# Layer norm's exact root on GpSimd instead of VectorE, and a new written order for all steps

## The chip, the cores and the metric

The kernel runs on one core of one Trainium2 chip. The metric is the device time of one execution in microseconds (us). Three runs of the kernel before took 794.92, 795.9 and 796.6 us; the median is 795.9 us.

Names used below: PE is TensorE (PEld its weight load), DVE is VectorE, ACT is ScalarE, POOL is GpSimd, SP is SyncE, whose queue issues nearly all the transfers of this kernel. A small q behind an engine's name (SPq) is its sequencer, which waits and issues.

## The reference

Inputs are q, k and v (8 x 8 heads x 576 x 64), a gain g of 512 and two matrices, 512 x 2048 and 2048 x 512.

```python
k_p = k.reshape(B, H, S // 8, 8, D).mean(axis=3)          # pooled keys and values
v_p = v.reshape(B, H, S // 8, 8, D).mean(axis=3)
scores = (q @ k_p.T) / sqrt(D);  attn = softmax(scores);  x = attn @ v_p
mu = mean(x);  var = mean((x - mu)**2)                     # rows of 512
xn = (x - mu) / np.sqrt(var + 1e-06) * g_ln                # layer norm
out = x + np.maximum(xn @ w_ch1, 0.0) @ w_ch2              # feed-forward
```

The random inputs give scores with a large spread (q and k are multiplied by 8), so float32 accuracy is kept: large products are made of float16 parts (high and low).

## The kernel before, in words

**Tiles and chunks.** The 4608 rows are 36 tiles of 128 rows; four tiles make a chunk of 512 rows, and there are nine chunks, 0 to 8. Scores, softmax and values of a tile are the steps A and B. The feed-forward of a chunk follows: for chunks 0 and 1 by plain products (steps I, lines 1083 to 1098, and O, lines 1118 to 1135), for chunks 2 to 8 by a Strassen scheme with seven products (steps U, whose matmuls are line 794, and E, whose matmuls are line 1017). The parts that these products read are made by ACT (high part) and by DVE or POOL (low part: source minus high part; lines 839 and 846 among others).

**The root.** Layer norm's 1/sqrt is found in two parts. For each tile the last part of step B (lines 627 to 644) makes the variance `ve_all` and a first guess `s_all` by integer arithmetic, and the row is scaled with the guess. The correction to the exact root, times the output scale, is found for four tiles at once by step NR (`norm_scale`, line 558): from 128x4 tiles, one instruction after the other, each reading what the one before it wrote, into `cr`. The second product's accumulation (lines 1033 and 1129, on DVE) multiplies by `cr`. So NR of a chunk may run at any time between the chunk's last step B and its first accumulation. In the kernel before NR has eight instructions on DVE (lines 563 to 580), in three pieces with a `yield` between.

**Low parts on POOL.** POOL makes part of the low parts (lines 545, 548, 679, 702, 846), half of the weight forms (lines 741, 744, 949, 952) and a conversion (line 347).

**Transfers.** SP's queue takes them in order. A doubled copy of the values (`va`, `vb`, lines 428 and 429, four transfers for each batch) is read by the matmuls of step B (lines 596 and 597). `vr` (line 405) and `kr` (line 401) have one buffer each, so a load waits until DVE has reduced the one before it (lines 1172 and 1148).

**The order.** Nothing is left to a scheduler: the string `START` is a list of 2486 tokens, and each token runs one step up to its next `yield`. `NR.4`, for one, appears three times in it: a piece each. Each engine's queue, and SP's, gets its instructions in the order in which the tokens issue them, and keeps to it; semaphores make an instruction wait for another engine's.

```python
    def step(token):
        if token not in begun:
            name, *args = token.split(".")
            begun[token] = iter(ops[name](*map(int, args)) or ())
        next(begun[token], None)

    with tc.manual_schedule():
        for token in START.split():
            step(token)
```

Of the kernel before, what the change touches and what calls it, by code (L numbers as in the profile page):

```python
# [63 lines left out]
C.2.0.1.1 K.1 V.1 K.1 C.1.4.1 K.1 K.1 B.2 B.3 K.1 C.2.0.1.1 C.1.4.1 R.1.5 K.1 A.4 S.1.2 C.1.4.1 V.1 A.4 C.2.0.1.1
R.2.6 S.1.3 S.1.3 A.5 B.2 C.1.4.1 C.1.5.1 C.1.5.1 A.4 B.2 B.3 I.0.0.0 A.4 B.3 C.1.5.1 A.4 B.2 I.0.0.0 HV.2.0 A.5 B.3
HK.2.0 C.2.6.1 C.2.6.1 R.2.2 B.2 C.1.5.1 A.5 A.4 HK.2.1 B.3 C.2.6.1 I.0.0.0 I.0.0.0 R.2.4 A.4 C.2.2.1.1 I.0.1.1
I.0.0.0 I.0.1.0 I.0.1.1 M1.1 M1.1 C.2.6.1 A.5 C.2.2.1.1 C.2.2.1.1 I.0.0.0 I.0.1.0 B.4 M1.1 V.1 A.5 I.0.1.1 S.1.4
C.2.2.1.1 I.0.0.0 A.6 A.6 I.0.1.0 V.1 I.0.1.0 I.0.0.0 B.4 I.0.1.0 C.2.4.1 A.6 I.0.1.1 I.0.1.1 S.1.4 S.1.5 I.0.0.0
I.0.0.1 I.0.0.1 R.2.3 V.1 C.2.3.1 I.0.1.0 HV.2.0 HK.2.1 A.5 A.5 A.6 S.1.5 I.0.0.1 I.0.0.1 I.0.0.1 C.2.3.1 R.2.5
C.2.3.1 QS.9 A.6 I.0.0.1 HK.2.0 C.2.4.1 C.2.4.1 I.0.1.1 A.7 I.0.1.1 I.0.1.1 S.1.6 I.0.1.1 C.2.3.1 S.1.6 I.0.0.1  # L70
I.0.0.1 I.0.1.1 HK.2.0 I.0.0.1 V.1 V.1 I.0.0.0 I.0.0.1 I.0.0.0 S.1.7 S.1.7 I.0.2 B.4 I.0.0.1 I.0.0.0 I.0.0.1 A.6
HV.2.1 HV.2.1 C.2.5.1.1 A.7 C.2.5.1.1 C.2.5.1.1 C.2.4.1 I.0.1.1 I.0.2 I.0.1.1 R.2.1 I.0.1.0 I.0.1.0 B.4 HK.2.1 HV.3.1
QS.9 I.0.2 C.2.5.1.1 A.7 T.0.0.1 HV.3.1 I.0.1.0 I.0.3 B.5 T.0.0.1 I.0.1.0 NR.0 I.0.3 R.2.7 C.2.1.1 C.2.1.1 I.0.3
I.0.1.0 T.0.0.1 B.5 C.2.7.1 B.4 I.0.2 I.0.2 I.0.3 C.2.1.1 B.4 A.6 C.2.7.1 C.2.7.1 T.0.0.1 C.2.1.1 I.0.1.0 HK.2.1 I.0.2
I.0.2 C.2.7.1 A.7 T.0.0.1 M2 X.0 I.0.2 T.0.0.1 HV.2.0 HV.2.0 X.1 M2 I.0.3 A.8 B.5 M2 I.0.3 I.0.2 S.2.0 A.8 I.0.2 B.4
I.0.2 S.2.0 KS.2 I.0.3 Y.0 T.0.0.1 HV.2.0 Y.1 A.7 S.2.1 I.0.2 S.2.1 I.0.3 S.2.2 KS.2 HV.2.0 I.0.3 S.2.2 X.2 HV.2.0
S.2.3 I.0.3 I.0.3 T.0.0.1 F.0.0.0 S.2.3 HV.2.0 I.0.3 Y.2 A.8 S.2.4 QS.9 QS.9 A.7 QS.10 KS.2 KS.2 NR.0 S.2.4 T.0.0.1
NR.0 B.5 B.6 HV.3.1 S.2.5 B.5 F.0.0.0 S.2.5 X.3 T.0.0.1 HV.3.1 HK.3.0 HV.3.1 QS.9 O.0.0 O.0.0 T.0.0.1 F.0.0.0 B.5 Y.3
F.0.0.0 O.0.0 QS.9 S.2.6 S.2.6 S.2.7 HV.3.1 KS.2 S.2.7 O.0.0 O.0.0 A.8 B.6 T.1.0.1 B.7 B.5 B.7 B.6 KS.2 HV.3.1 A.8 B.7
T.1.0.1 O.0.0 B.6 QS.10 T.0.0.1 B.7 HV.3.1 QS.10 B.6 B.6 N.1.1 F.0.0.0 O.0.0 QS.10 QS.10 B.7 O.0.1 A.9 O.0.1 A.9 A.9  # L80
A.8 HV.2.1 B.6 B.7 B.7 F.0.0.0 B.4 QS.12 HK.3.0 QS.10 HV.2.1 HK.3.0 T.0.0.1 A.9 F.0.0.0 HV.2.1 F.0.0.0 O.0.1 O.0.1
O.0.1 O.0.1 F.0.0.0 F.0.0.0 O.0.0 O.0.1 HV.2.1 F.0.0.0 B.8 HV.2.1 A.10 A.10 QS.11 I.1.0 A.9 I.1.0 O.0.1 A.10 HV.2.1
HV.2.1 B.8 T.1.0.1 T.1.0.1 A.9 HK.3.0 I.1.3 I.1.0 F.0.1.1 HV.2.1 F.0.1.1 HV.3.0 A.10 T.1.0.1 I.1.2 F.0.0.0 HV.2.1
HV.3.0 QS.11 QS.11 HK.3.1 O.0.1 O.0.1 HV.3.0 QS.11 F.0.1.1 HK.3.1 HV.3.0 HK.3.1 F.1.0.1 F.1.0.1 T.1.0.1 I.1.3 B.8
I.1.3 I.1.2 QS.11 I.1.3 F.1.0.1 I.1.2 A.10 NR.1 HV.2.1 I.1.3 HV.3.0 HV.3.0 I.1.3 QS.11 F.1.0.1 F.1.0.1 N.0.1 F.1.0.1
I.1.1 A.10 F.1.0.1 HV.2.1 HV.2.1 T.1.0.1 HK.3.1 N.1.3 O.0.1 O.0.1 I.1.3 F.1.0.1 KS.3 I.1.3 A.11 A.11 I.1.0 F.0.1.1
I.1.3 A.11 QS.12 HV.3.0 KS.3 KS.3 I.1.1 A.11 QS.12 I.1.1 QS.13 I.1.1 B.8 QS.12 QS.12 B.10 B.10 F.1.0.1 KS.3 F.1.0.1
HV.3.0 NR.1 T.1.0.1 I.1.0 A.11 I.1.0 F.1.0.1 QS.13 I.1.1 QS.13 I.1.0 I.1.1 I.1.0 I.1.0 I.1.2 I.1.3 KS.3 F.1.1.0 A.11
I.1.2 I.1.2 F.1.1.0 QS.13 B.10 T.1.0.1 KS.3 F.1.0.1 T.1.0.1 F.1.1.0 HV.4.1 I.1.0 I.1.0 I.1.1 B.8 QS.13 F.2.0.0 F.2.0.0
F.1.1.0 I.1.1 B.9 B.9 B.8 I.1.3 HV.4.1 B.9 I.1.1 I.1.1 QS.12 T.0.1.1 N.0.2 I.1.0 NR.1 HV.4.1 I.1.2 B.9 A.12 T.0.1.1  # L90
QS.13 F.2.0.0 A.12 N.1.0 T.1.0.1 A.12 HV.4.1 I.1.1 B.11 B.9 QS.15 I.1.3 I.1.2 I.1.1 T.0.1.1 HV.4.1 QS.14 T.1.0.1 B.10
B.9 F.2.0.0 O.1.0 F.2.0.0 HV.4.1 I.1.2 A.12 A.13 I.1.2 B.11 B.8 QS.14 QS.14 B.9 O.1.0 B.9 F.2.0.0 F.2.0.0 HK.4.0 QS.14
HV.4.1 B.9 B.9 A.12 QS.14 B.11 HK.4.0 F.2.0.0 QS.14 B.9 HV.3.1 HK.4.0 F.2.0.0 F.2.0.0 HV.4.1 QS.15 O.1.0 HV.4.0 A.12
O.1.0 B.11 F.2.0.0 I.1.2 T.1.0.1 T.1.1 B.9 QS.15 QS.15 N.0.3 O.1.0 A.14 O.1.0 B.9 HV.4.0 O.1.0 NR.2 F.2.1.1 HV.4.0
QS.15 QS.15 B.11 T.0.1.1 I.1.2 HK.4.0 O.1.1 B.10 QS.16 B.10 B.11 F.2.1.1 B.11 A.13 A.13 F.2.1.1 B.10 F.2.1.1 O.1.1
HK.4.1 O.1.1 O.1.1 F.3.0.1 B.12 U.2.0.1 T.1.1 B.11 B.11 O.1.0 A.14 NR.2 HV.4.0 F.3.0.1 HK.4.1 F.2.0.0 B.11 B.11 O.1.1
B.12 A.13 F.3.0.1 N.1.2 F.3.0.1 F.3.0.1 HV.4.0 QS.16 B.11 T.1.1 O.1.1 HV.3.1 HV.3.1 O.1.1 O.1.1 B.12 B.11 F.3.0.1
T.0.1.1 O.1.1 F.3.0.1 HV.4.0 U.2.0.1 B.12 F.3.0.1 HK.4.1 T.1.1 F.3.0.1 F.3.0.1 T.1.1 QS.16 QS.16 A.15 F.3.0.1 A.13
O.1.1 U.2.0.6 O.1.1 HK.4.1 U.2.0.6 U.2.0.6 U.2.0.2 U.2.0.5 U.2.0.7 F.3.0.1 U.2.0.2 F.3.1.0 QS.16 HV.3.1 U.2.0.2 A.13
HV.4.0 N.0.0 U.2.0.5 U.2.0.3 U.2.0.7 U.2.0.4 HV.3.1 U.2.1.1 NR.2 U.2.0.3 U.2.0.7 A.14 U.2.1.1 HV.3.1 U.2.0.7 U.2.1.6  # L100
A.14 B.13 HV.4.0 J.1.0 U.2.0.4 U.2.0.3 U.2.1.6 B.13 U.2.2.1 J.0.1 U.2.0.3 F.3.1.0 F.3.1.0 D.2.0.0 U.2.1.6 U.2.0.4
U.2.0.3 U.2.0.4 HV.4.1 U.2.1.2 U.2.0.3 U.2.1.7 QS.17 U.2.1.5 F.3.1.0 U.2.2.1 U.2.1.2 U.2.1.2 U.2.2.2 B.13 U.2.1.5
HV.5.0 HK.5.0 A.15 U.2.1.3 U.2.1.7 U.2.1.4 U.2.0.4 U.2.0.4 U.2.0.4 J.0.0 QS.16 B.12 U.2.1.3 HV.4.1 HV.5.0 KS.4 HV.4.1
U.2.0.4 U.2.1.3 E.2.0.1 U.2.1.7 U.2.1.4 U.2.1.3 E.2.0.1 U.2.1.4 U.2.2.6 KS.4 U.2.2.6 KS.4 A.14 D.2.0.1 U.2.1.4 U.2.1.4
KS.4 A.14 E.2.0.2 E.2.0.2 A.16 QS.18 HV.5.0 U.2.1.4 E.2.0.6 U.2.2.5 O.1.1 A.15 U.2.1.4 U.2.1.4 U.2.2.6 D.2.0.2 QS.17
QS.17 QS.17 U.2.1.3 KS.4 U.2.2.2 QS.17 B.13 U.2.2.7 U.2.2.2 A.15 QS.18 HK.5.0 J.1.1 U.2.1.3 U.2.2.5 B.13 E.2.0.6 B.14
E.2.0.5 A.16 E.2.0.6 D.2.0.3 U.2.2.7 U.2.2.4 U.2.2.7 QS.18 A.15 A.15 HK.5.1 A.16 B.12 B.14 B.14 U.2.2.4 U.2.2.3 QS.18
QS.18 B.13 E.2.0.7 B.15 U.2.2.7 U.2.2.3 U.2.2.4 U.2.1.7 E.2.0.5 U.2.3.1 U.2.2.4 U.2.3.1 HV.4.1 E.2.0.3 U.2.3.6 HK.5.1
# [1260 lines left out]
```

## Time and profile before

| | us |
|---|---|
| three runs | 794.92, 795.9, 796.6 |
| the profiled execution | 795.79 |
| its span (first to last instruction) | 794.0 |
| PE busy | 769.4 (97%) |
| DVE busy | 683.0 (86%) |
| ACT busy | 501.7 (63%) |
| POOL busy | 322.0 (41%) |

The span is 1.8 us shorter than the execution's own time. Matmul ends are modelled, so PE's busy time is not all peak work. A group's row in a list by line and form gives the line, engine, operation, output and inputs, shapes and count, then the busy time (us) and the mean duration (ns), then the idle time of the engine just before and what ended it. A mean that is larger than that of a sister group with the same shape is time in which the instruction had started and was held up.

### The profile page before, as it was taken

How to read it: one execution, taken by the hardware profiler on the slowest of the kernel's cores; microseconds unless marked ns; L12 is line 12 of the kernel's file. 1: busy time of each engine (PE TensorE's matmuls, PEld its weight loads, DVE VectorE, ACT ScalarE, POOL GpSimd, SP SyncE). 2: the span in 40 equal slices, each digit the busy share in tenths (PEclk: the TensorE clock that was granted, in tenths of full speed). 3: DMA queues.
4: the chain of work that ended last, by engine and by line, in shares of the span. 5: the costliest groups of instructions: out<-in, count | busy, mean ns of one | idle time of the engine just before them, and what ended most of it. 6: DMA issues, size and time to landing. Idle time of an engine off the chain costs nothing.

```text
span 794.0 us, 17760 instructions
## 1 busy us (share of the span) xinstructions
PE 769.4 (97%) x6904; PEld 618.0 (78%) x6904; DVE 683.0 (86%) x1439; ACT 501.7 (63%) x963; POOL 322.0 (41%) x282
## 2 busy tenths in 40 slices
...
GB/s 332 355 276 272 227 279 219 216 196 128 137 199 192 279 136 207 193 181 145 177 158 220 91 182 163 177 138 176 208 89 154 111 140 127 118 148 89 27 108 120
DMA packets 248356, 140.72 MB, mean 177 GB/s; under 512 B 158112, under 2 KB 225680, under 8 KB 245200
## 3 DMA queue, kind: packets, MB, share of 16 engines
...
q10 hardware_dynamic: 144, 0.13, 0.0%
...
## 4 chain that ended last, share of the span: by engine, by line
PE 70%; DVE 22%; DMA 3%; ACT 2%; issue 2%; SPq 1%; POOL 0%; DVEq 0%; ACTq 0%
PE ps_f L1017 29%; PE ps_f L794 28%; PE ps_f L1083 4%; DMA vr<-in_v_dram 2%; DVE vp L1172 1%; DVE w L315 1%; PE ps_f L1118 1%; PE ps_f L1272 1%; PE ps L486 1%; DVE w L353 1%; DVE ring L1097 1%; DMA w<-in_vn_dram 1%; PE ps_f L1256 1%; PE ps L594 1%; DVE ring L846 1%
## 5 line engine op out<-in xcount | busy, mean ns | idle before, releaser
L1017 PE MATMUL ps_f<-w,ring 128*128 128x256 f16 x2352 | 267.6, 273 | 4.3 <-DVE ring L839 1.9
L1017 PEld LDWEIGHTS <-ring 128*128 128x128 f16 x2352 | 229.0, 98 | 31.9 <-issue 4.3
L794 PE MATMUL ps_f<-zz,w 128*128 128x256 f16 x1344 | 160.6, 273 | 0.0
L794 PEld LDWEIGHTS <-w 128*128 128x128 f16 x1344 | 130.5, 98 | 15.0
L846 POOL TENSOR_TENSOR ring<-v,ring 128x512 f16<-128x512 f32 x56 | 67.0, 1200 | 166.1 <-ACT ring L843 149.1
L794 PE MATMUL ps_f<-zz,raw 128*128 128x256 f16 x1008 | 121.8, 273 | 0.5 <-DVE v L902 0.4
L794 PEld LDWEIGHTS <-raw 128*128 128x128 f16 x1008 | 97.7, 98 | 12.5 <-issue 0.6
L1083 PE MATMUL ps_f<-zz,w 128*128 128x512 f16 (+1 forms) x480 | 88.8, 344 | 3.6 <-DVE ring L1097 3.6
L1118 PE MATMUL ps_f<-w,ring 128*128 128x512 f16 x384 | 84.8, 379 | 0.7 <-DVE ring L1097 0.4
L1083 PEld LDWEIGHTS <-w 128*128 128x128 f16 x480 | 47.3, 100 | 39.4 <-issue 6.2
L1118 PEld LDWEIGHTS <-ring 128*128 128x128 f16 x384 | 36.9, 98 | 45.2 <-DVE ring L1097 1.3
L846 POOL TENSOR_TENSOR ring<-ring 128x512 f16<-128x512 f32 x28 | 34.7, 1241 | 66.4 <-ACT ring L843 49.3
L545 POOL TENSOR_TENSOR phl<-e,phl 128x512 f16<-128x512 f32 x31 | 38.0, 1224 | 50.9 <-ACT phl L537 46.1
L702 POOL TENSOR_TENSOR hl<-z,hl 128x512 f16<-128x512 f32 x28 | 32.7, 1176 | 54.2 <-ACT hl L700 44.5
L622 ACT ACTIVATE x<-ps,rs 128x64 f32<-128x64 f32 x144 | 33.1, 316 | 10.8 <-DVE x L614 10.5
L843 ACT CAST ring<-v 128x512 f16<-128x512 f32 x56 | 34.5, 618 | 5.7 <-DVE v L852 3.9
L843 ACT CAST ring<-ring 128x512 f16<-128x512 f32 x56 | 34.0, 618 | 3.0 <-PE ps_f L1017 2.9
L1172 DVE TENSOR_REDUCE vp<-vr 72x64 f32<-72x512 f32 x48 | 32.3, 674 | 3.1 <-DMA vr<-in_v_dram 3.1
L869 ACT COPY ps_f<-w 128x512 f32<-128x512 f32 x28 | 16.5, 589 | 28.2 <-DVE w L867 28.2
L537 ACT CAST phl<-e 128x1024 f16<-128x1024 f32 x31 | 32.4, 1046 | 2.3 <-DMA pt<-phl 1.3
L1033 DVE SCALAR_TENSOR_TENSOR x<-ps_f,cr,x 128x256 f32<-128x256 f32 x58 | 25.3, 476 | 9.4 <-PE ps_f L1017 9.4
L644 ACT ACTIVATE z<-x,nb,s_all 128x512 f32<-128x512 f32 x36 | 29.2, 815 | 5.9 <-DVE nb L639 5.6
...
## 6 DMA issues: line engine op xcount, KB each, us to landing
...
```

The source lines that it names most:

```text
L537: nc.scalar.copy(out=ph[:, :, :, 0:KA], in_=e[:, :, 0:KA].unsqueeze(1).broadcast_to([P, 2, H, KA]))
L545: nc.gpsimd.tensor_tensor(out=ph[:, 0, :, KA:P], in0=e[:, :, 0:KA], in1=ph[:, 0, :, 0:KA], op=ALU.subtract)
L622: nc.scalar.activation(out=xh[:, 4 + i, :], in_=px[:, 1, i, 0:D], func=AF.Copy, scale=rs[:, 4 + i : 5 + i])
L644: nc.scalar.activation(out=z, in_=x, func=AF.Identity, scale=y, bias=nb)
L702: nc.gpsimd.tensor_tensor(out=hl[:, 1, r], in0=part, in1=hl[:, 0, r], op=ALU.subtract)
L794: nc.tensor.matmul(ps[:, j], lhsT=w_form(wb, int(m == 2), k)[:, fs], rhs=z_form(za, int(m == 1), k), start=(first and i == 0 and j == 0), ...
L843: nc.scalar.copy(out=hi, in_=src)
L846: eng.tensor_tensor(out=lo, in0=src, in1=hi, op=ALU.subtract)
L1017: nc.tensor.matmul(parts[i], lhsT=h[:, hp, f, i * P : (i + 1) * P], rhs=w[:, f // FPB, wp, f % FPB], start=(first and f == k == 0 and (i = ...
L1083: nc.tensor.matmul(ps, lhsT=w[:, part, fs], rhs=zT[:, kz, cols], start=(n == 0), stop=(n == 3 * NKT - 1),)
L1118: nc.tensor.matmul(ps, lhsT=h[:, part, i, cols], rhs=w[:, wp, j], start=(n == 0), stop=(n == 3 * NFT // 2 - 1),)
L1172: nc.vector.tensor_reduce(out=vp[b][:, h, 0:D], in_=vraw.pop((b, h)), axis=AX.X, op=ALU.add,)
```

## The change: NR's arithmetic on POOL, and a new START

The function `norm_scale` issues on POOL what it issued on DVE. [...] The three pieces stay (three, three and four instructions instead of three, two and three). Nine steps NR make 90 POOL instructions. `START` has the same 2486 tokens, each as often as before, in another order over its whole length.

```diff
-LK.0 K.0 Q.1 Q.0 K.0 LV.0 A.1 A.1 A.1 R.1.1 A.1 A.0 R.1.3 V.0 A.1 A.1 G A.0 A.0 V.0 A.0 V.0 C.1.1.0.1 V.0 Q.2 V.0 V.0
+Q.1 LK.0 K.0 K.0 Q.0 LV.0 A.1 A.1 A.1 A.0 A.0 A.1 V.0 A.1 V.0 V.0 A.1 V.0 V.0 R.1.1 C.1.1.0.1 C.1.1.0.1 R.1.3 A.0
...
-        nc.vector.tensor_tensor(out=a, in0=v, in1=y, op=ALU.mult)
-        nc.vector.scalar_tensor_tensor(
-            out=a, in0=a, scalar=2.0 ** (-2 * Z_EXP), in1=y, op0=ALU.mult, op1=ALU.mult
-        )
-        nc.vector.tensor_scalar(
-            out=d, in0=a, scalar1=-0.5, scalar2=1.5, op0=ALU.mult, op1=ALU.add
-        )
-        yield
-        nc.vector.tensor_tensor(out=u, in0=d, in1=d, op=ALU.mult)
-        nc.vector.tensor_tensor(out=u, in0=u, in1=a, op=ALU.mult)
-        yield
-        nc.vector.scalar_tensor_tensor(
-            out=a, in0=u, scalar=10.0 / 3.0, in1=u, op0=ALU.subtract, op1=ALU.mult
-        )
-        nc.vector.scalar_tensor_tensor(
-            out=a, in0=a, scalar=5.0, in1=d, op0=ALU.add, op1=ALU.mult
-        )
-        nc.vector.tensor_scalar(
-            out=cr[:, r], in0=a, scalar1=0.375, scalar2=c_out, op0=ALU.mult, op1=ALU.mult
-        )
+        tt, ts = nc.gpsimd.tensor_tensor, nc.gpsimd.tensor_scalar
+        k = 2.0 ** (-2 * Z_EXP)
+        tt(out=a, in0=v, in1=y, op=ALU.mult)
+        tt(out=a, in0=a, in1=y, op=ALU.mult)
+        ts(out=d, in0=a, scalar1=-0.5 * k, scalar2=1.5, op0=ALU.mult, op1=ALU.add)
+        yield
+        tt(out=u, in0=d, in1=d, op=ALU.mult)
+        tt(out=u, in0=u, in1=a, op=ALU.mult)
+        ts(out=a, in0=u, scalar1=k, scalar2=-10.0 / 3.0, op0=ALU.mult, op1=ALU.add)
+        yield
+        tt(out=a, in0=a, in1=u, op=ALU.mult)
+        ts(out=a, in0=a, scalar1=k, scalar2=5.0, op0=ALU.mult, op1=ALU.add)
+        tt(out=a, in0=a, in1=d, op=ALU.mult)
+        ts(out=cr[:, r], in0=a, scalar1=0.375, scalar2=c_out, op0=ALU.mult, op1=ALU.mult)
```

Behind `norm_scale` every line number of the changed kernel is smaller by 6 (line 846 is 840 there, 1033 is 1027). Three places of the queues follow. In them `m_5243` and `t_5244` (before), `m_5308`, `m_5310` and `t_5309` (changed) are the small tiles of NR.4, and `cr` its result.

DVE's queue before, around the third piece of NR.4 (lines 574, 577 and 580):

```order
L839 SCALAR_TENSOR_TENSOR ring<-v,ring 128x512
L852 SCALAR_TENSOR_TENSOR v<-v,zz 128x512
L902 TENSOR_TENSOR v<-ps_f,v 128x512
L1033 SCALAR_TENSOR_TENSOR x<-ps_f,cr,x 128x256 x2
L574 SCALAR_TENSOR_TENSOR m_5243<-m_5245 128x4
L577 SCALAR_TENSOR_TENSOR m_5243<-m_5243,t_5244 128x4
L580 TENSOR_SCALAR cr<-m_5243,c_out 128x4
L517 TENSOR_TENSOR e<-ps_5484,mx 128x576
L846 TENSOR_TENSOR ring<-ring 128x512
```

The three small instructions stand in DVE's queue between the work of two products; in the changed kernel none of NR is left in this queue.

POOL's queue of the changed kernel, the second and third piece of NR.4:

```order
L840 TENSOR_TENSOR ring<-v,ring 128x512
L569 TENSOR_TENSOR m_5310<-t_5309 128x4
L570 TENSOR_TENSOR m_5310<-m_5310,m_5308 128x4
L571 TENSOR_SCALAR m_5308<-m_5310 128x4
L840 TENSOR_TENSOR ring<-v,ring 128x512
L573 TENSOR_TENSOR m_5308<-m_5308,m_5310 128x4
L574 TENSOR_SCALAR m_5308<-m_5308 128x4
L575 TENSOR_TENSOR m_5308<-m_5308,t_5309 128x4
L576 TENSOR_SCALAR cr<-m_5308,c_out 128x4
L840 TENSOR_TENSOR ring<-v,ring 128x512
```

The small instructions stand between POOL's low parts (line 840 here, 846 before); in the kernel before POOL's queue has none of NR.

SP's queue around the doubled values of batch 2, before:

```order
L405 DMA vr<-in_v_dram 72x512
L472 DMA_TRANSPOSE q<-q 128x8x128
L963 DMA d2T_1315<-v 128x1024
L941 DMA d2B_1852<-w_88 128x4x256
L556 DMA_TRANSPOSE pt<-phl_108 128x16x128
L428 DMA va<-vh 64x520
L429 DMA vb<-vh 8x520
L428 DMA va<-vh 64x520
L429 DMA vb<-vh 8x520
```

and in the changed kernel:

```order
L405 DMA vr<-in_v_dram 72x512
L556 DMA_TRANSPOSE pt<-phl_108 128x16x128
L957 DMA d2T_1498<-v 128x1024
L405 DMA vr<-in_v_dram 72x512
L453 DMA q<-in_qn_dram 128x512
L428 DMA va<-vh 64x520
L429 DMA vb<-vh 8x520
L428 DMA va<-vh 64x520
L429 DMA vb<-vh 8x520
```

There a load of `vr`, which waits for a reduction on DVE (line 1166 of the changed kernel), now stands just ahead of the four transfers.

## Rows read from the trace of the kernel before

**Rows 1.** Windows: stretch, length, busy us (xcount) of PE PEld DVE ACT POOL, clock, DMA share, GB/s.

```profile
20.00:100.00 80.00, 73.62 (x501) 56.26 (x501) 74.52 (x144) 71.03 (x125) 35.13 (x24) 0.85 0.85 282
100.00:240.00 140.00, 138.30 (x841) 67.13 (x840) 128.81 (x258) 75.42 (x144) 93.04 (x66) 1.00 0.77 196
240.00:480.00 240.00, 235.50 (x2411) 207.99 (x2411) 225.07 (x503) 163.94 (x324) 92.54 (x88) 1.00 0.78 178
480.00:620.00 140.00, 139.69 (x1459) 125.35 (x1458) 125.90 (x283) 95.32 (x193) 47.88 (x47) 1.00 0.70 160
```

**Rows 2.** Waits of PE, 100 to 480 us: us in total, times, longest.

```profile
PE ps_f L1017 <- DVE ring L839: 1.9, 2, 1.0
PE ps_f L1017 <- DVE x L1033: 1.0, 1, 1.0
PE ps_f L1017 <- ACT v L1049: 0.9, 1, 0.9
PE ps_f L299 <- DVE rowmax L277: 0.8, 1, 0.8
...
```

**Rows 3.** Lines by form, DVE, 100 to 480 us: NR's eight instructions.

```profile
L571 DVE TENSOR_TENSOR m<-t 128x4 f32<-128x4 f32 x5 | 4.6, 922 | 0.0
L580 DVE TENSOR_SCALAR cr<-m,c_out 128x4 f32<-128x4 f32 x5 | 3.7, 739 | 0.2
L564 DVE SCALAR_TENSOR_TENSOR m<-m,s_all 128x4 f32<-128x4 f32 x5 | 3.0, 604 | 0.2
L567 DVE TENSOR_SCALAR t<-m 128x4 f32<-128x4 f32 x5 | 2.7, 537 | 0.2
L574 DVE SCALAR_TENSOR_TENSOR m<-m 128x4 f32<-128x4 f32 x5 | 2.2, 432 | 0.0
L563 DVE TENSOR_TENSOR m<-ve_all,s_all 128x4 f32<-128x4 f32 x5 | 2.2, 431 | 0.0
L572 DVE TENSOR_TENSOR m<-m,m 128x4 f32<-128x4 f32 x5 | 0.8, 163 | 0.2
L577 DVE SCALAR_TENSOR_TENSOR m<-m,t 128x4 f32<-128x4 f32 x5 | 0.8, 163 | 0.2
```

**Rows 4.** Timeline of DVE at 89, 179 and 726 us: start, length, instruction.

```profile
89.53 0.99 DVE L567 TENSOR_SCALAR t<-m 128x4 f32<-128x4 f32 x1
...
179.28 1.84 DVE L571 TENSOR_TENSOR m<-t 128x4 f32<-128x4 f32 x1
...
725.96 0.15 DVE L571 TENSOR_TENSOR m<-t 128x4 f32<-128x4 f32 x1
```

**Rows 5.** Timeline of POOL, 178 to 183 us.

```profile
178.97 2.13 POOL L741 TENSOR_TENSOR raw<-w,raw 128x1024 f16<-128x1024 f32 x1
```

**Rows 6.** Lines by form, POOL, whole span.

```profile
L846 POOL TENSOR_TENSOR ring<-v,ring 128x512 f16<-128x512 f32 x56 | 67.0, 1200 | 166.1 <-ACT ring L843 149.1 <-DVE m L574 8.7 <-DMA va<-vh 8.2
...
L548 POOL TENSOR_TENSOR phl<-e,phl 128x64 f16<-128x64 f32 x31 | 12.6, 406 | 0.0
...
L250 POOL MEMSET kp_all<- 128x16 f32 x1 | 0.1, 111 | 0.0
```

**Rows 7.** Lines by form, DVE, whole span: first and last of its groups, and line 846.

```profile
L1172 DVE TENSOR_REDUCE vp<-vr 72x64 f32<-72x512 f32 x48 | 32.3, 674 | 3.1 <-DMA vr<-in_v_dram 3.1
...
L846 DVE TENSOR_TENSOR ring<-ring 128x512 f16<-128x512 f32 x28 | 24.8, 887 | 0.5 <-ACT ring L843 0.5
...
L846 DVE TENSOR_TENSOR ring<-zz,ring 128x512 f16<-128x512 f32 x15 | 10.3, 687 | 1.5 <-ACT ring L843 1.4
...
L1276 DVE MEMSET vp<- 72x8 f32 x2 | 0.1, 65 | 0.0
```

**Rows 8.** Instructions of lines 428 and 429 (SP): ns min/median/max, first and last start.

```profile
L428 SPq DMA_DIRECT2D va<-vh x14: 504/516/804, 70.9 to 603.5; - x14
...
L429 SPq DMA_DIRECT2D vb<-vh x14: 670/715/852, 71.5 to 604.0; - x14
```

**Rows 9.** Chain that ended last, 100 to 260 us: start, us, a transfer's part.

```profile
175.03 3.63 DMA vr<-in_v_dram
```

More of the change, by code (lines that the diff above doesn't have):

```diff
@@ L64 @@
[L64 to L108, printed above, removed]
@@ new lines @@
+V.1 HK.2.0 S.1.3 R.2.6 HK.2.1 C.1.5.1 C.1.4.1 C.1.4.1 C.1.4.1 S.1.3 A.4 A.4 I.0.0.0 B.2 C.1.5.1 I.0.0.0 C.2.6.1
+I.0.1.0 B.3 I.0.1.0 A.4 A.4 C.2.6.1 I.0.0.0 C.1.5.1 B.2 I.0.1.0 A.5 I.0.1.0 C.1.5.1 C.2.6.1 A.4 NR.0 V.1 A.5 I.0.1.0
+I.0.1.0 I.0.0.0 A.4 B.4 R.2.2 B.2 C.2.6.1 A.5 A.5 B.2 I.0.1.1 HV.2.0 HK.2.1 C.2.2.1.1 R.2.3 C.2.2.1.1 I.0.0.0 HV.2.0
+M1.1 C.2.2.1.1 A.5 M1.1 M1.1 I.0.1.1 I.0.1.1 A.5 R.2.4 I.0.0.0 I.0.1.1 A.6 A.6 V.1 I.0.1.1 A.6 C.2.3.1 I.0.1.1 I.0.0.0
+A.6 S.1.4 C.2.4.1 C.2.2.1.1 S.1.4 B.4 C.2.3.1 C.2.3.1 I.0.1.0 I.0.1.0 I.0.1.0 I.0.0.1 C.2.4.1 I.0.0.1 I.0.0.1 S.1.5
@@ new lines @@
+A.5 S.1.5 I.0.0.1 I.0.0.1 I.0.0.0 A.6 HK.2.0 HV.2.1 I.0.0.1 C.2.4.1 S.1.6 I.0.0.1 HV.2.1 I.0.0.0 A.7 S.1.6 I.0.1.1
+I.0.0.1 A.7 I.0.1.1 I.0.1.1 I.0.0.1 A.6 I.0.0.1 R.2.5 C.2.3.1 HV.3.1 S.1.7 S.1.7 I.0.0.0 I.0.0.1 QS.9 R.2.1 I.0.0.0
+B.4 V.1 I.0.3 C.2.4.1 HV.3.1 I.0.0.0 C.2.5.1.1 B.4 C.2.5.1.1 C.2.5.1.1 C.2.1.1 I.0.1.1 HK.2.0 V.1 I.0.3 I.0.2 I.0.3
+B.5 R.2.7 I.0.0.1 B.5 QS.9 T.0.0.1 I.0.1.1 I.0.2 C.2.1.1 I.0.1.1 I.0.2 HV.2.0 I.0.1.0 HK.2.1 X.0 T.0.0.1 C.2.7.1
+C.2.7.1 C.2.5.1.1 I.0.2 I.0.1.0 HV.2.0 HV.2.0 A.7 I.0.2 I.0.1.0 T.0.0.1 T.0.0.1 T.0.0.1 T.0.0.1 C.2.1.1 C.2.1.1
@@ new lines @@
+C.2.7.1 I.0.2 I.0.2 C.2.7.1 A.8 HK.2.1 T.0.0.1 B.4 A.6 A.7 M2 QS.9 QS.9 X.1 Y.0 I.0.3 M2 M2 I.0.3 I.0.3 S.2.0 I.0.3
+I.0.3 HV.2.0 B.5 KS.2 S.2.0 I.0.2 QS.10 S.2.1 A.7 I.0.2 I.0.2 I.0.3 I.0.2 S.2.1 Y.1 QS.9 I.0.2 I.0.3 S.2.2 I.0.3 KS.2
+HV.2.0 S.2.2 F.0.0.0 S.2.3 S.2.3 HK.3.0 I.0.3 A.8 A.8 B.4 T.0.0.1 A.7 QS.9 S.2.4 S.2.4 HV.2.0 KS.2 B.5 A.8 S.2.5
+T.0.0.1 T.0.0.1 KS.2 X.2 B.5 KS.2 B.6 B.6 X.3 HV.3.1 S.2.5 HV.3.1 NR.0 F.0.0.0 O.0.0 O.0.0 O.0.0 Y.2 S.2.6 S.2.6 S.2.7
+O.0.0 F.0.0.0 O.0.0 B.7 B.7 B.7 HV.3.1 B.6 S.2.7 O.0.0 O.0.0 B.7 Y.3 A.8 B.5 B.7 B.4 HV.3.1 T.1.0.1 B.6 N.0.0 KS.2
@@ new lines @@
+B.11 HV.4.0 O.1.1 HV.4.0 A.13 B.11 B.10 B.11 A.12 T.1.1 A.13 O.1.0 O.1.0 O.1.0 T.0.1.1 F.2.0.0 B.11 B.12 O.1.1 B.12
+O.1.0 B.12 T.1.1 B.11 F.2.1.1 F.3.0.1 QS.15 F.3.0.1 F.3.0.1 T.0.1.1 B.12 HV.4.0 U.2.0.1 HV.4.0 QS.15 A.13 O.1.1 B.11
+T.1.1 O.1.1 F.3.0.1 U.2.0.1 HK.4.1 B.12 A.13 HV.3.1 O.1.1 HK.4.1 HV.4.0 HV.3.1 O.1.1 QS.15 A.14 U.2.0.2 QS.15 F.3.0.1
+F.3.0.1 U.2.0.2 O.1.1 O.1.1 QS.18 F.3.0.1 N.0.3 F.3.0.1 QS.16 F.3.0.1 F.3.0.1 T.1.1 U.2.0.6 U.2.0.6 F.3.0.1 A.14
+HV.4.0 HV.4.1 HK.4.1 O.1.1 U.2.0.2 U.2.0.6 N.1.3 HV.5.0 A.14 A.15 U.2.0.5 U.2.0.7 HV.3.1 F.3.0.1 NR.2 U.2.0.5 KS.4
```

223 lines of the change are left out of this document (124 added, 99 removed).

## The prediction, made before the changed kernel ran

> **What bounds the kernel now.** I read the windows by stage first, then PE's waits, then the groups of DVE and POOL by line and form, and last the order of both kernels. The windows show a kernel that TensorE bounds: from 480 to 620 us PE is busy 139.69 of 140 us, and before that it is short of full by 80 - 73.62 = 6.4 us (20 to 100 us), 140 - 138.30 = 1.7 us (100 to 240) and 240 - 235.50 = 4.5 us (240 to 480) [rows 1]. The reader should see next to it how full DVE is: 128.81 of 140 and 225.07 of 240 us, 92 and 94%; where it falls to 125.90 of 140, 90%, PE's idle time is gone [rows 1]. PE's waits between 100 and 480 us name DVE first: 1.9 us for line 839, 1.0 for line 1033, 0.8 for line 277; one of the four longest is ACT's, 0.9 [rows 2]. So the matmuls, the same in both kernels, set some 97% of the time. What a change of DVE's and POOL's queues can give is the 6.2 us that PE idles between 100 and 480 us, part of the 6.4 us before 100, and little else.
>
> **What leaves DVE.** NR's eight instructions on 128x4 tiles cost DVE 4.6 + 3.7 + 3.0 + 2.7 + 2.2 + 2.2 + 0.8 + 0.8 = 20.0 us between 100 and 480 us [rows 3]. Four elements don't take that long. The two groups that were never held mean 163 ns, line 571 922 ns [rows 3]; late in the run line 571 takes 0.15 us, but at 179.28 us it takes 1.84 us, to 181.12 [rows 4], and POOL's instruction that began at 178.97 and took 2.13 us ends at 181.10 [rows 5]. A small DVE instruction that meets a running POOL instruction waits until that one ends. So most of the 20.0 us is waiting, and it goes with the instructions. In the changed order, what does DVE's queue hold ahead of the same amount of matmul work? I added the queue up, in the two orders, with each group's mean duration (105 groups, the first 48 x 674 ns, the last 2 x 65 ns [rows 7]). Up to where PE has done some 85 us of matmul work the queue is 1.5 us shorter, at 120 us 5, at 350 us 12, at 422 us 19.8. This is what NR gives up and no more; the new order neither brings other DVE work forward nor puts it off on balance. The sums overlap at their ends, so only the difference between the orders is used.
>
> **What DVE gets back.** POOL runs 90 more instructions, 50 of them for the five steps that lie in that stretch. Their length isn't in the trace. From below it is the 16-column memset, 111 ns; from above the 128x512 part, 1200 ns; the nearest is the 128x64 subtraction, 406 ns [rows 6]. I take 0.3 us, nearer to the 128x64 row than to the memset. That is 27 us on an engine that is busy 93.04 + 92.54 of 380 us [rows 1], so POOL has room (10 to 108 us by the two ends). Each may hold up a DVE instruction for up to its length. On average I take half, 0.15 us: 50 x 0.15 = 7.5 us come back, and DVE is relieved of 20.0 - 7.5 = 12.5 us. By the ends it is 20.0 - 50 x 0.11 = 14.5 us, or, with every one held by a 1.2 us instruction, 40 us worse. The Trainium skill ("SBUF — State Buffer", section "Who interferes with whom") says the pair of ports is an exclusive lock for the whole instruction, and that issue order decides who blocks. The trace agrees for DVE behind POOL, as above; for POOL behind DVE it speaks against this change, since a small POOL instruction would then wait out a long DVE one. That is part of the slower rival below.
>
> **The sum, 100 to 480 us.** PE's idle time there is 6.2 us. The waits for ACT's line 1049 (0.9) and for line 277 (0.8, a maximum's chain of small steps) I leave, since they are latency; 4.5 us go. Term: -4.5 us, between 0 (the relief goes into DVE's own idle time, 380 - 128.81 - 225.07 = 26.1 us) and -6.2 (all of it).
>
> **The sum, before 100 us.** The last instruction of NR.0's first piece, line 567, cost 0.99 us at 89.53 us [rows 4], and the piece stands in DVE's queue in the stretch that holds the 6.4. Here ACT's queue is as long as DVE's and in the new order 0.5 us longer at that place, and the first transfers change places by one load of q. Term: -1.0 us, that one instruction, between -2 (twice it, since line 563 of the piece may wait as long) and +1. If NR.0's pieces on POOL, which wait for the last variance of the chunk on DVE, hold up the three conversions of line 347 behind them, that is the +1.
>
> **What the order costs.** SP's four transfers of the doubled values of batch 2 stand in the new order behind a load of `vr` that waits for a reduction on DVE. That reduction comes 0.67 us of DVE work [rows 7] after the instruction that PE itself awaits, 2.4 us of matmuls before it needs the values. From the reduction on it takes two issues ahead of them (0.5 us each as an estimate, from line 428's least), 2 x (0.516 + 0.715) = 2.5 us for the four issues [rows 8], and a landing, at most the 3.6 us of the `vr` transfer in the chain [rows 9]; I take 2.0 since these are smaller. 0.67 + 1.0 + 2.5 + 2.0 - 2.4 = 3.8 us, if DVE is just in time there; but its queue is 5 us shorter by then, so it should be ahead. Term: +0.3, between 0 and +3.8. `cr` of chunk 4 is the tightest result of NR: its four last instructions stand 3.9 us of DVE work ahead of their reader. At 0.3 us each they need 1.2 us; with a wait of 0.69 us for a DVE instruction before each (line 846's free mean [rows 7]) 4.0 us. Term: 0, at most +0.1. The other readers stand 5 us or more of matmuls later.
>
> Sum: -4.5 - 1.0 + 0.3 = -5.2 us from the profiled execution's 795.8 (span 794.0 and 1.8 around it; the median of the runs is 0.1 above). Forecast 790.6 us. Its own range is 787 to 794.
>
> **Rivals.** (1) POOL gives the port back dearer than it took it: slower. Place: the 50 POOL instructions between 100 and 480 us, each waiting for a DVE instruction and then holding the next. It decides from a length of 20.0 / 50 = 0.40 us per held DVE instruction on: then DVE has won nothing, while the transfers of batch 2 (+3.8) and a `cr` that is late by 0.5 us stay. 795.8 + 3.8 + 0.5 = 800.1 us. For it speaks that the 128x64 row means 406 ns; against it that a 128x4 instruction is shorter, and that DVE's instruction is then one of up to 0.7 us (line 846's free mean), which only delays POOL, and POOL has room. Chance 0.14. (2) The relief goes into DVE's idle time: PE's waits are chains through ACT and back, and the 26.1 us that DVE idles only grow. Only the waits for lines 839 and 1033 shrink by half, 1.5 us, and +0.3 is paid: 794.6 us. For it speaks that DVE is idle 6% of that stretch already. Chance 0.13. (3) The new order also takes port waits away from work that stays on DVE. Line 846 means 887 ns where its sister means 687: 28 x 0.2 = 5.6 us over the run [rows 7]. Then all of the 6.2 us between 100 and 480 us goes and about half of the 6.4 us before 100: 795.8 - 6.2 - 3.2 = 786.4 us. Whether the new order does this can't be read from it. Chance 0.23.
>
> **How the numbers follow.** The forecast has 0.50. A difference under 0.2%, 1.6 us, can't be told from no change by a measurement of this kernel: faster is under 794.3, slower over 797.5. Faster: nearly all of the forecast (0.48), rival 3 (0.23) and a third of rival 2 (0.04): 0.75. Same: the rest of rival 2 and a little of the others, 0.10. Slower: rival 1 and the tail of the forecast, 0.15. The range for 8 in 10 reaches from 783.5, beyond rival 3 because a matmul's end is modelled and a shorter wait can lie under it unseen, to 798.0, short of rival 1.
>
> **What would show it.** In the changed kernel's profile DVE should be some 25 us less busy over the run, and lines 563 to 580 gone from it. POOL should have ten new groups with x9, some 0.3 us each; at 0.4 us or more and with DVE's groups (line 840 of the changed kernel above all) longer than before, rival 1 is on its way. PE's idle time between 100 and 480 us should fall from 6.2 to about 2 us; if it stays over 4 while DVE idles more than 30 us, it is rival 2. A PE wait for `va` or `vb` near 165 us is the price of SP's order. Before 100 us PE should idle 5 to 6 us. The prediction is wrong if PE's matmuls issue slower by themselves, or if the clock that TensorE is granted differs by more than the 0.85 of 20 to 100 us [rows 1].

## The result, and the profile after

| | before | changed |
|---|---|---|
| median of four runs each, us | 795.51 | 786.32 |
| lowest and highest, us | 794.92, 796.6 | 784.12, 787.19 |

The ratio of the times is 0.9879, with a 95% interval of 0.9855 to 0.9902. A second set of runs gave 0.9884 (0.9863 to 0.9905). The changed kernel is faster by some 9 us, where 5.2 were forecast. Times of different sets are compared below by such ratios; a gain in us is (1 - ratio) x 795.5. One execution, the profiled one of the sixth experiment, took 1615.55 us, twice the rest, and nothing is read from it.

The page's first part of the changed kernel, busy time of each engine, answers to the table of before (DVE 683.0 us, POOL 322.0):

```profile
PE 765.9 (98%) x6904; PEld 616.2 (78%) x6904; DVE 655.5 (83%) x1367; ACT 500.2 (64%) x963; POOL 349.1 (44%) x372
```

DVE lost 27.5 us and 72 instructions, POOL gained 27.1 us and 90. The windows of the changed kernel (columns as in [rows 1]):

```profile
20.00:100.00 80.00, 74.33 (x533) 57.17 (x532) 71.36 (x149) 72.80 (x128) 36.59 (x30) 0.91 0.88 291
100.00:240.00 140.00, 138.87 (x854) 68.59 (x853) 126.97 (x246) 77.66 (x146) 104.87 (x85) 1.00 0.81 200
240.00:480.00 240.00, 239.13 (x2472) 212.64 (x2470) 215.99 (x479) 164.51 (x330) 98.55 (x119) 1.00 0.81 182
480.00:620.00 140.00, 140.00 (x1464) 125.80 (x1463) 122.53 (x273) 95.05 (x190) 53.30 (x65) 1.00 0.66 151
```

PE's idle time from 100 to 480 us was 1.7 + 4.5 us; it is 1.1 + 0.9 = 2.0. Before that (20 to 100 us) it was 6.4 us and is 5.7. A second profile of the changed kernel has 1.1 us in the later stretch and 3.3 us in the first, and 652.2 us of DVE instead of 655.5, so differences of this size between single profiles are scatter. PE's waits from 100 to 480 us, all of them, against the longer list that [rows 2] begins:

```profile
PE ps_f L1011 <- DVE x L1027: 0.9, 1, 0.9
PE ps_f L1112 <- DVE x L1123: 0.7, 1, 0.7
PE ps_f L1112 <- DVE w L315: 0.2, 1, 0.2
```

The root on POOL, lines by form, whole span, against the DVE groups of [rows 3]:

```profile
L569 POOL TENSOR_TENSOR m<-t 128x4 f32<-128x4 f32 x9 | 3.6, 401 | 0.2
L573 POOL TENSOR_TENSOR m<-m,m 128x4 f32<-128x4 f32 x9 | 3.2, 358 | 0.0
L576 POOL TENSOR_SCALAR cr<-m,c_out 128x4 f32<-128x4 f32 x9 | 2.7, 304 | 1.0
L574 POOL TENSOR_SCALAR m<-m 128x4 f32<-128x4 f32 x9 | 2.6, 294 | 0.8
L575 POOL TENSOR_TENSOR m<-m,t 128x4 f32<-128x4 f32 x9 | 2.6, 284 | 0.8
L570 POOL TENSOR_TENSOR m<-m,m 128x4 f32<-128x4 f32 x9 | 2.5, 276 | 0.7
L566 POOL TENSOR_TENSOR m<-m,s_all 128x4 f32<-128x4 f32 x9 | 1.8, 198 | 0.7
L565 POOL TENSOR_TENSOR m<-ve_all,s_all 128x4 f32<-128x4 f32 x9 | 1.8, 197 | 3.6 <-DVE s_all L625 3.6
L567 POOL TENSOR_SCALAR t<-m 128x4 f32<-128x4 f32 x9 | 1.7, 194 | 0.8
L571 POOL TENSOR_SCALAR m<-m 128x4 f32<-128x4 f32 x9 | 1.7, 193 | 0.8
```

They sum to 24.2 us, 0.27 us each (0.3 was taken). Four groups mean 193 to 198 ns; the others are longer by waits. For the price of SP's order, PE's one wait for the doubled values, in the first 100 us of the changed kernel, is

```profile
PE ps L590 <- DMA va<-vh: 0.3, 1, 0.3
```

and PE waits for nothing near 165 us.

### The profile page after: what moved, and what is told of

Read it like the earlier page. It is cut to its first block, busy times and chain, and to the rows that moved or that the text cites. A ratio compares the mean times of both kernels' runs of the same rounds, so it can differ in the third digit from the quotient of the medians.

```text
span 785.5 us, 17760 instructions
## 1 busy us (share of the span) xinstructions
PE 765.9 (98%) x6904; PEld 616.2 (78%) x6904; DVE 655.5 (83%) x1367; ACT 500.2 (64%) x963; POOL 349.1 (44%) x372
## 4 chain that ended last, share of the span: by engine, by line
PE 79%; DVE 10%; ACT 4%; DMA 4%; issue 1%; POOL 1%; SPq 1%; DVEq 0%; ACTq 0%; POOLq 0%
PE ps_f L1011 31%; PE ps_f L788 30%; PE ps_f L1112 6%; PE ps_f L1077 6%; DVE w L315 2%; PE ps L486 2%; PE ps_f L1250 1%; PE ps L590 1%; PE ps L494 1%; DMA raw<-in_w_dram 1%; DMA zz<-hl 1%; PE ps L591 1%; DMA vr<-in_v_dram 1%; DMA w<-in_kT_dram 1%; DVE mx L508 1%
## 5 line engine op out<-in xcount | busy, mean ns | idle before, releaser
L696 POOL TENSOR_TENSOR hl<-z,hl 128x512 f16<-128x512 f32 x28 | 34.3, 1234 | 59.2 <-ACT hl L694 59.2
L526 ACT ACTIVATE e<-e,qe 128x576 f32<-128x576 f32 x27 | 20.9, 773 | 19.5 <-DVE e L517 19.5
```

What stands on the lines that cost most here:

```text
L696: nc.gpsimd.tensor_tensor(out=hl[:, 1, r], in0=part, in1=hl[:, 0, r], op=ALU.subtract)
```

## The experiments

**1 to 4: the order and the move, apart and by stretch.** The first two take one half of the change each:

```diff
 # order alone: the kernel before, with the new START
-LK.0 K.0 Q.1 Q.0 K.0 LV.0 ...
+Q.1 LK.0 K.0 K.0 Q.0 LV.0 ...
 # move alone: the changed kernel, with the START of before
-Q.1 LK.0 K.0 K.0 Q.0 LV.0 ...
+LK.0 K.0 Q.1 Q.0 K.0 LV.0 ...
```

The other two have the root on POOL and join 290 tokens of one START to what is left of the other:

```python
START = new[:290] + [tokens of old not yet used]    # third
START = old[:290] + [tokens of new not yet used]    # fourth
```

Order alone, expected:

> The changed kernel's order of steps with layer norm's root left on DVE (the eight instructions of before). Theory M (the move takes the port waits off DVE between 100 and 480 us; the order gives about 3 us before 100 us and nothing later): PE idles about 6 us between 100 and 480 us as before, about 792.5 us (790.5 to 794.5). Rival O (the new order by itself takes the port waits away, as rival 3 of the prediction had it): PE's idle time there falls to 3 us or less without the move, 787 to 790 us. Rival P (the order was found for a queue without these steps and is worse with them): 795 us or more.

Measured: 790.77 us, ratio 0.9938 (0.9919 to 0.9957). Windows of the order alone:

```profile
100.00:240.00 140.00, 136.85 (x840) 67.20 (x838) 129.82 (x254) 76.42 (x145) 97.35 (x69) 1.00 0.77 194
240.00:480.00 240.00, 238.86 (x2461) 211.53 (x2459) 222.00 (x502) 163.10 (x326) 92.00 (x88) 1.00 0.80 182
```

PE idles 3.15 + 1.14 = 4.3 us there: less than before (6.2), more than in the changed kernel. The time lies at the lower end of theory M's range, 0.8 us over rival O's, but the sign that M gave, 6 us of idle time there, is missing, and so is O's, 3 us or less: the order does gain after 100 us by itself, but only part.

Move alone, expected:

> The order of before with the ten steps on POOL. Theory M: DVE is some 25 us less busy, PE's idle time between 100 and 480 us falls from 6.2 to about 2 us, the first 100 us stay as before: 795.5 - 4.5 = 791 us (789.5 to 792.5). Rival O: the move gives little without the order, 793.5 us or more. A third way: POOL's queue of before makes the root late (its steps stand behind low parts that wait for ACT), PE or DVE waits for cr, 794 us or more.

Measured: 788.58 us, 0.9915 (0.9885 to 0.9944): better than theory M. Windows and the first part of the page of the move alone:

```profile
20.00:100.00 80.00, 76.92 (x528) 59.66 (x528) 72.68 (x148) 74.16 (x133) 35.44 (x27) 0.87 0.87 293
100.00:240.00 140.00, 139.70 (x860) 67.91 (x859) 120.64 (x250) 75.43 (x141) 108.44 (x92) 1.00 0.79 201
240.00:480.00 240.00, 238.78 (x2473) 213.91 (x2472) 218.85 (x479) 165.69 (x332) 99.11 (x117) 1.00 0.82 181
```

```profile
PE 768.1 (98%) x6904; PEld 619.1 (79%) x6904; DVE 651.6 (83%) x1367; ACT 500.9 (64%) x963; POOL 352.4 (45%) x372
```

The reader should see two things. PE's idle time falls to 1.5 us after 100 us and from 6.4 to 3.1 us before, so the move gains in both stretches, with the old order, where theory M had left the first 100 us as they were. And DVE falls to 651.6 us. NR's eight groups on DVE were 31.8 us over the whole run before, and 683.0 - 31.8 = 651.2. What was left on DVE became 0.4 us longer: in this profile almost nothing is given back (two profiles of one kernel differ by up to 3.3 us in this number).

Start of the changed kernel, then the old order, expected and measured (785.67 us, 0.9882, 0.9853 to 0.9912):

> Root on POOL; the first 290 of the 2486 tokens (some 95 us) in the changed kernel's order, the rest in the order of before. Theory M: both gains, 795.5 - 3 - 4.5 = 788 us (786.5 to 789.5), 3 us under the kernel with the move alone. Rival O (the later order matters): 790 us or more, since the rest has the old order. If the first 95 us are worth nothing, it equals the move alone.

The reverse, expected and measured (786.71 us, 0.9895, 0.9867 to 0.9922):

> Root on POOL; the first 290 tokens in the order of before, the rest in the changed kernel's order. Theory M: the changed kernel's 786.3 plus the 3 us that its first 95 us gain: 789.3 us (788 to 790.5), and TensorE's granted clock near 0.85 instead of 0.91 between 20 and 100 us. Rival O: 787 us or less, since all the gain lies in the later order.

Both are as fast as the changed kernel within their intervals. Both are also faster than the move alone, which ran in the same set: by the means of six runs each, the new start ahead of the old order by 2.6 us (95%: 0.9 to 4.3), the new order behind the old start by 1.6 us (0.1 to 3.0). So either part of the new order gives some of its gain, and the whole of it no more than the start does. Neither theory holds in both: the third lies 3 us under the move alone, as theory M had it, though below M's range, and the fourth lies in rival O's.

**5, 6 and 9: chunk 0's root apart from the others.** The kernel and order of before; `norm_scale` is one or the other, and the ninth is the sixth's kernel again:

```diff
+    def norm_scale(c):
+        return norm_scale_pool(c) if c == 0 else norm_scale_dve(c)    # sixth and ninth: c > 0
```

> The order of before; only chunk 0's root (NR.0) on POOL, the other eight on DVE. Theory N (term B was sized wrong: the whole first piece of NR.0, 2.1 us at 88.4 us, and what it delays up to 100 us stand on the path): PE waits 2.8 us less near 95 us, 795.8 - 3 = 793 us (791.5 to 794.3), and PE idles about 6 us between 100 and 480 us as before. Rival S (the first 100 us differ by chance from run to run, the piece is worth the 1.0 us of the forecast or less): 794.5 us or more.

> The order of before; NR.1 to NR.8 on POOL, NR.0 on DVE. Theory N: term A alone, PE's idle time between 100 and 480 us falls from 6.2 to 2 us or less and the PE wait near 95 us stays: 795.8 - 4.6 = 791.2 us (790 to 792.5); this gain and that of NR.0 alone add up to the 7.6 us of the move alone. Rival S: all of the 7.6 us come from here, 789 us or less.

> The order of before, NR.1 to NR.8 on POOL and NR.0 on DVE, once more, for a profile that can be read. Theory N: 791 us (790 to 792.5); PE idles 2 us or less between 100 and 480 us, and PE's wait of 2 to 3 us for the feed-forward's low part near 95 us is there as in the kernel before.

Measured: NR.0 alone 791.58 us, 0.9954 (0.9935 to 0.9973), a gain of 3.7 us (2.1 to 5.2). The other eight 791.37 and 791.06 us, 0.9952 twice (0.9934 to 0.9970; 0.9932 to 0.9972), a gain of 3.8 us (2.4 to 5.3). The sum, 7.5, agrees with the move alone (6.8, 4.5 to 9.1). Eight of the nine steps are worth what the first one is worth. Theory N holds, and the traces show why. DVE of the kernel before (start, length, instruction):

```profile
88.03 0.41 DVE L1097 SCALAR_TENSOR_TENSOR ring<-ps_f,ring 128x256 f16<-128x256 f32 x1
88.36 0.94 DVE L563 TENSOR_TENSOR m<-ve_all,s_all 128x4 f32<-128x4 f32 x1
89.34 0.17 DVE L564 SCALAR_TENSOR_TENSOR m<-m,s_all 128x4 f32<-128x4 f32 x1
...
90.42 0.68 DVE L1097 SCALAR_TENSOR_TENSOR ring<-ps_f,ring 128x512 f16<-128x512 f32 x1
...
91.85 4.29 DVE L353 SCALAR_TENSOR_TENSOR w<-w,raw 128x1024 int32<-128x1024 int32 x2
96.06 0.41 DVE L1097 SCALAR_TENSOR_TENSOR ring<-ps_f,ring 128x256 f16<-128x256 f32 x1
```

and with NR.0 alone on POOL (line 1097 is 1120):

```profile
89.26 1.01 DVE L1120 SCALAR_TENSOR_TENSOR ring<-ps_f,ring 128x256 f16<-128x256 f32 x2
...
91.01 1.32 DVE L353 SCALAR_TENSOR_TENSOR w<-w,raw 128x1024 int32<-128x1024 int32 x1
93.38 1.23 DVE L353 SCALAR_TENSOR_TENSOR w<-w,raw 128x1024 int32<-128x1024 int32 x1 [1.04 <-POOL raw L347]
94.52 0.42 DVE L1120 SCALAR_TENSOR_TENSOR ring<-ps_f,ring 128x256 f16<-128x256 f32 x1
```

Before, the piece puts 2.06 us (88.36 to 90.42) between two low parts, ahead of the one at 96.06 us, for which PE waits. Then the two `L353` come later, beside a long POOL instruction that had begun when the second of them came:

```profile
92.49 2.57 POOL L741 TENSOR_TENSOR raw<-w,raw 128x1024 f16<-128x1024 f32 x1 [1.99 <-ACT raw L750]
```

The second of them starts at 93.0 us and takes 3.16 us, where the median of its kind is 1.22. The two take 4.29 us; with NR.0 on POOL they and the wait between them take 3.60 (91.01 to 94.61). So the piece itself is most of the delay and the collision adds 0.7: 2.06 + 0.69 = 2.75 us. PE of the kernel before, and its window:

```profile
93.13 0.60 PE L655 MATMUL ps_f<-ident,z 128*128 128x128 f32 x4
96.53 4.27 PE L1083 MATMUL ps_f<-zz,w 128*128 128x512 f16 x12 [2.80 <-DVE ring L1097]
```

```profile
95.00:100.00 5.00, 3.47 (x10) 1.25 (x10) 4.18 (x10) 3.03 (x5) 4.84 (x3) 0.66 0.59 197
```

with NR.0 on POOL:

```profile
94.35 0.60 PE L678 MATMUL ps_f<-ident,z 128*128 128x128 f32 x4
94.99 2.75 PE L1106 MATMUL ps_f<-zz,w 128*128 128x512 f16 x12
```

```profile
95.00:100.00 5.00, 5.00 (x28) 2.85 (x28) 4.72 (x14) 4.90 (x12) 4.84 (x3) 1.00 0.85 275
```

and with the other eight there and NR.0 on DVE (the ninth):

```profile
97.77 4.04 PE L1106 MATMUL ps_f<-zz,w 128*128 128x512 f16 x12 [2.85 <-DVE ring L1120]
```

A wait of 2.80 us goes, and twelve matmuls behind it take 2.75 us instead of 4.27; the granted clock of the stretch is 1.00 instead of 0.66. That is 2.80 + 1.52 = 4.3 us in this place; the timed runs show 3.7. In the ninth both are back (2.85 and 4.04 us). The windows of NR.0 alone and of the other eight, 100 to 480 us:

```profile
100.00:240.00 140.00, 138.19 (x852) 67.05 (x851) 126.64 (x256) 75.39 (x140) 101.40 (x75) 1.00 0.78 198
240.00:480.00 240.00, 235.20 (x2410) 208.55 (x2409) 224.38 (x498) 164.38 (x325) 91.71 (x89) 1.00 0.78 178
```

```profile
100.00:240.00 140.00, 138.95 (x845) 67.58 (x844) 123.14 (x251) 76.64 (x146) 100.57 (x82) 1.00 0.77 199
240.00:480.00 240.00, 237.78 (x2438) 210.65 (x2436) 217.72 (x478) 165.54 (x327) 103.65 (x120) 1.00 0.79 180
```

NR.0 alone leaves PE's idle time there at 6.6 us; the other eight bring it to 3.3, above the 2 that was expected.

**7: the price of a small POOL instruction.** The changed kernel, each step issued three times, twice into a tile that nobody reads:

```diff
-        tt, ts = nc.gpsimd.tensor_tensor, nc.gpsimd.tensor_scalar
+        def thrice(f):
+            def g(out, **kw):
+                f(out=j, **kw); f(out=j, **kw); f(out=out, **kw)
+            return g
+        tt, ts = thrice(nc.gpsimd.tensor_tensor), thrice(nc.gpsimd.tensor_scalar)
```

> The changed kernel with each of the 90 small instructions of the root issued three times on POOL (the first two of each into a tile that nobody reads): POOL some 49 us busier. Theory M (small POOL instructions hardly hold DVE, POOL has room): PE idles 2 to 4 us between 100 and 480 us, 787.5 us (786 to 789). Rival 1 of the prediction (each POOL instruction is paid back on the port): at three times 0.27 us for each step the price is over the 0.40 us from which it decides, 795 us or more. Between the two, at half of each length paid back (0.13 us for each of the 100 added between 100 and 480 us): 13 us on DVE, 790 to 792 us.

Measured: 789.58 us, 0.9942 (0.9920 to 0.9963). The first part of its page:

```profile
PE 766.1 (97%) x6904; PEld 615.1 (78%) x6904; DVE 661.0 (84%) x1367; ACT 500.7 (64%) x963; POOL 407.2 (52%) x552
```

180 more instructions add 58 us to POOL and 5.5 us to DVE (8.8 against the changed kernel's second profile), 0.03 to 0.05 us each, and cost 3.3 to 5.4 us (by medians and by ratios, against both sets of the changed kernel). The median lies between theory M's range and the half-length's, the ratio (790.9 us) in the half-length's; but the 13 us on DVE that go with the half-length's are not there. Rival 1 falls. It also bounds what the 90 real ones can cost: if it grows evenly, 1.6 to 2.7 us.

**8 and 12: PE's clock in the first 60 us.** Ten tokens more in START, each a pair of unread matmuls; in the twelfth, in the order of the third:

```diff
-... V.1 A.2 C.1.0.1 A.2 A.2 ...
+... W.0 W.1 W.2 V.1 A.2 C.1.0.1 A.2 W.3 W.4 A.2 ...
```

> The changed kernel with ten pairs of matmuls that nobody reads (128x512, into ps_f) put where PE idles between 24 and 41 us. Theory C (PE's idle time there is why the clock is granted at half between 42 and 55 us, and that stretch lies on the path): the clock stays at 1.00 there and 3 to 5 us go, 782 to 783.5 us. Rival D (in the first 60 us PE waits for transfers and DVE anyway, or the clock falls all the same): 786 us or more, up to 2 us slower by the added matmuls.

> Root on POOL, first 290 tokens in the changed kernel's order, the rest in the order of before, and the ten pairs of unread matmuls between 24 and 41 us: the two small gains seen so far (785.7 and 785.0 us) together. If both are real and add up: 784.4 us (783 to 785.5). If they were scatter: 786 us, as the changed kernel.

Measured: 785.00 us, 0.9891 (0.9866 to 0.9915), and 788.17 us, 0.9930 (0.9906 to 0.9954). The clock in the eighth:

```profile
45.00:50.00 5.00, 5.00 (x25) 4.68 (x27) 4.79 (x12) 4.29 (x8) 2.85 (x5) 0.50 0.31 103
```

It falls to half all the same (0.50 there in the changed kernel too), as rival D had it, so what that stretch costs was not measured, and what sets it stays open. The 785.00 us lie between the two forecasts; by the ratio it is 786.8 us, in rival D's. The twelfth fits neither of its forecasts: by the means of its set it is 3.3 us (1.0 to 5.5) slower than the changed kernel, so the two do not add up, and why it is slower stays open. No version beat the changed kernel.

**10: the changed kernel again.**

> The changed kernel again, beside the others of this set: 786.3 us (784 to 787.5) by its first runs.

Measured: 784.15 us, 0.9884 (0.9863 to 0.9905).

**11: only the root's places in the order.** Root on DVE, all else as before, NR's 27 tokens moved:

```diff
 # NR.0 at these counts of other tokens (the other chunks alike)
-281 363 365
+124 164 378
```

> The kernel before, root on DVE, all other steps in the order of before; only the 27 tokens of NR stand at the places (by count of the other tokens) that they have in the changed kernel's order. Theory V (the order alone gains 5.4 us because NR's pieces stand where POOL holds them less: NR's DVE instructions 31.8 us before, 21.9 with the order alone): 791 us (789.5 to 792.5), NR's instructions some 22 us. Rival W (the gain of the order lies in the order of the other steps): 794.5 us or more. Half of each: 793 us.

Measured: 792.54 us, 0.9975 (0.9959 to 0.9991). Two of NR's eight groups on DVE, whole span, in the kernel before, with the order alone, and with the moved root:

```profile
L567 DVE TENSOR_SCALAR t<-m 128x4 f32<-128x4 f32 x9 | 6.0, 669 | 0.3
L580 DVE TENSOR_SCALAR cr<-m,c_out 128x4 f32<-128x4 f32 x9 | 4.6, 513 | 0.3
```

```profile
L567 DVE TENSOR_SCALAR t<-m 128x4 f32<-128x4 f32 x9 | 3.4, 380 | 0.3
L580 DVE TENSOR_SCALAR cr<-m,c_out 128x4 f32<-128x4 f32 x9 | 2.1, 229 | 0.3
```

```profile
L567 DVE TENSOR_SCALAR t<-m 128x4 f32<-128x4 f32 x9 | 3.3, 363 | 0.3
L580 DVE TENSOR_SCALAR cr<-m,c_out 128x4 f32<-128x4 f32 x9 | 2.1, 230 | 0.3
```

All eight sum to 31.8, 21.9 and 21.7 us. So the new places alone take away 10 us of NR's own waiting, and gain 2.0 us (0.7 to 3.3) of the 4.9 (3.4 to 6.4) that the order alone gains. Theories V and W hold about half each. Little of the 2.0 us lies between 100 and 480 us: PE's idle time there is 5.7 us instead of 6.2, though the root's instructions in that stretch fell from 20.0 to 11.9 us. What its profile does show is a change at the place of NR.0. The window there, with the order alone and with the moved root (0.66 before):

```profile
95.00:100.00 5.00, 5.00 (x25) 2.31 (x24) 3.51 (x15) 4.78 (x9) 4.84 (x3) 1.00 1.00 352
95.00:100.00 5.00, 3.81 (x22) 2.16 (x21) 4.50 (x11) 4.50 (x11) 4.84 (x3) 1.00 0.98 349
```

In both profiles PE's wait of 2.80 us for the low part is gone, as it is with NR.0 on POOL. So order and move remove one wait in common, which would explain why they give 4.9 + 6.8 = 11.7 us apart and 9.2 to 9.6 together; but the intervals are too wide to show that the sum differs.

## Why the prediction came out as it did

- **What bounds, and the direction: right, with a part left out.** PE is 98% busy, and most of the gain is idle time of PE that DVE caused. But the span fell by 8.5 us, and 3.5 of them are PE's busy time, 769.4 to 765.9 us for the same 6904 matmuls. The granted clock between 20 and 100 us rose from 0.85 to 0.91 (0.89 in the second profile). The prediction named a change of this clock as a sign of being wrong and has it at nothing in its sum. Part of it is the stretch at 95 us (0.66 to 1.00). The rest is not told apart: between 20 and 30 us the two profiles of the changed kernel differ (1.00 and 0.66).
- **Term A, 100 to 480 us (-4.5): right within its range.** PE's idle time fell by 4.2 us with the whole change (5.1 in the second profile) and 2.9 in the ninth; the eight steps alone gain 3.8 us (2.4 to 5.3). That the rest would be the waits for ACT's line 1049 and for line 277 was wrong: both are gone, and what is left are other waits, mostly for DVE's accumulation (lines 1027 and 1123). So it is partly luck that 4.5 comes so close. And the 12.5 us of relief did not lead to it: in the eleventh DVE was relieved of 8.1 us there, and PE's idle time fell by 0.5.
- **What DVE gets back (0.15 us for each POOL instruction): too dear.** The move alone left 0.4 us on DVE over 90 instructions, and tripling them added 0.03 to 0.05 us each. POOL's means of up to 401 ns, against 193 to 198, show that it waits in turn; it is 44% busy and has room. The term did no harm, because term A was taken from PE's idle time. The Trainium skill ("Perfetto Trace Analysis", section "Optimizing Scalar/DVE Operations") warns that moving work between DVE and GpSimd might not help, as they share a port. Here it helps: the move alone is worth 6.8 us.
- **Term B, before 100 us (-1.0): this is the step that failed.** It took one instruction of NR.0's first piece, 0.99 us. But the whole piece, 2.06 us, stood ahead of a low part that PE waits for, pushed a conversion into a long POOL instruction (0.7 us more), and the wait of 2.8 us that came of it was followed by a lower clock. NR.0 alone is worth 3.7 us (2.1 to 5.2), beyond the -2 that the term allowed.
- **Term C, the order's cost (+0.3): no cost seen, and the sign may be wrong.** No wait for `va` or `vb` near 165 us. From the move alone (0.9915) to the whole (0.9879 and 0.9884) the order adds 2 to 3 us of gain, though the intervals overlap. Where in the order this lies is open beyond the third and fourth experiments. The sums of DVE's queue with mean durations could not show that, since a mean hides which instruction was held.
- **Rival 3 (786.4 us) had the number but not the reason.** What stays on DVE is not lighter: 683.0 - 31.8 = 651.2 us before, 655.5 and 652.2 in the changed kernel's two profiles. Its sign, line 846, did move (ring<-ring 887 to 732 ns, ring<-zz 687 to 738), and other lines took it back. Rivals 1 and 2 fall: the price of a small POOL instruction is small, and PE's idle time did go.

The forecast of 5.2 us was under the 9 measured because of term B, the clock behind it and the order.

With the measured terms, -3.8 (A) - 3.7 (B) and 2 to 3 for the order, the sum is 9.5 to 10.5 us, which gives 785 to 786 us, against 786.3 and 784.2 measured. The intervals of the terms are some 3 us wide, so this agreement shows little by itself.
